# A fused attention and gated MLP on one core: each engine's order worked out in the kernel by a list schedule, with fixed buffers and output stores on the sync engine

## The chip, the cores and the metric

The kernel runs on one core of one Trainium2 chip. Its engines each work through a queue of their own, in order: TensorE (PE) with its weight loads (PEld), VectorE (DVE), ScalarE (ACT), GpSimd (POOL) and SyncE (SP), which only issues transfers here. They wait for each other by semaphores. The metric is the device time of the whole program in microseconds (us), the median of the runs; 770.14 us before the change.

## The reference

```python
xn = layernorm(A_x)                          # 2048 tokens x 1024, bfloat16
qkv = xn @ wqkv                              # 32 heads of 32
# each token sees itself and 7 earlier ones, 2 apart (positions below 0 masked)
s = softmax(q . k_window * 32**-0.5) @ v_window @ wo
g = silu((silu(xn @ w1) * (xn @ w3)) @ w2)   # w1, w3: 1024 x 3584, w2: 3584 x 1024
out = A_x + s * g
```

## The kernel before

The 2048 tokens are four chunks c of 512 (`CH`), in two halves b of two chunks each. One half goes through: projections `qkv(c0)`, the MLP's first layer `mlp_up` in 14 steps fb of 256 hidden columns, with `attention(c0)`, `qkv(c1)` and `attention(c1)` put in among them, then the second layer `mlp_down`, then `wo(c0)`. `wo(c1)` of the first half comes after `qkv(2)` of the second.

- **LayerNorm.** Rows of x are normalised on DVE (`ln_norm`) or on ACT (`ln_norm_act`), transposed by PE (`ln_tp`, banks `tp`) and copied to `xT`.
- **Projection.** `qkv` takes three weight pairs of 2 x 1 MB (`wt`) and makes 8 banks of 8 matmuls from each; ACT evicts them to `qo`, `kT` and `vT`. `kT` and `vT` hold one chunk and 16 older columns, which POOL copies over (the halo) once the attention of the chunk before no longer reads them.
- **MLP.** Both layers use Strassen's scheme in Winograd's form on 2 x 2 blocks: seven products where eight would be needed, with sums of inputs (`xn_sums`, and the down stage's `s1t` to `s4t`), of weights (`w_sums`, `w2_sums`, made on DVE in the first half, stored to `s_dram` and `t_dram` by POOL's queue and loaded again later) and of products. In an up step PE runs groups of four matmuls into banks `ua`, `ue`, `ub`: two of each block product; ACT copies `ua` to a fresh bank (`fork`) and banks to buffers (`snap`); DVE adds, and multiplies gate by value. The last product of each pair, the *tail*, waits in `pend` and is run by `flush()` after the next step's first two products (or directly, at the end of a run of steps). DVE's `h_sb` sum of line 383 has to be through with the bank before the tail adds to it.
- **Attention.** DVE multiplies q by shifted k (`p_t`) and adds over 4 x 2 blocks into `E`; 16 small transfers from POOL's queue regroup `E` into `L` (line 244); DVE and ACT make the softmax (`z`, `zm`, `zs`, `pb`); 16 more transfers bring `pb` back into `E` (line 264); DVE multiplies by shifted v and adds, into `qo`.
- **Down.** `mlp_down` forms seven products per group g of 128 tokens in banks `da`, `db`, `de`: with w2's blocks (`w`) and its stored sums `T1` to `T4`. In the first half, ACT normalises the next half's x (`ln_norm_act`) and PE transposes it between products.
- **Output.** `wo` runs 8 matmuls a group, DVE multiplies by the gate (`o_t`, line 541) and adds x (`x_e`, line 542), and ACT's queue stores the result (line 543).

The buffers are rotating pools: six of 8 KB a partition (`r8`) for all weights and x, three (`att`) for attention, eight of 2 KB (`k2`), and all eight PSUM banks. The framework's scheduler sets the order of each engine's queue from the program order, with `tc.high_priority()` and `tc.issue_after` as hints, at build time. When a buffer comes free decides when a load can be issued: a load on SP waits for the last reader of its buffer, and everything behind it on SP waits too. A step's loads are asked for one step ahead (`up_load(b, fb + 1)`), also by the last step ahead of `qkv(c1)`.

Of the kernel before, what the change touches and what calls it, by code (L numbers as in the profile page):

```python
# [8 lines left out]
FP32 = mybir.dt.float32  # L9
# [4 lines left out]
AX = mybir.AxisListType  # L14
# [3 lines left out]
def kernel(  # L18
# [11 lines left out]

# [24 lines left out]
    NR = 4  # L55
    scale = float(Dh) ** -0.5
# [8 lines left out]

# [4 lines left out]
    psum = ctx.enter_context(tc.tile_pool(name="psum", bufs=8, space=bass.MemoryType.PSUM))  # L70
    small = ctx.enter_context(tc.tile_pool(name="small", bufs=4))
    keep = ctx.enter_context(tc.tile_pool(name="keep", bufs=1))
# [7 lines left out]
    eps_t = const.tile([P, 1], FP32, name="eps_t")  # L80
    nc.vector.memset(eps_t[:], 1e-5)
    scr = const.tile([P, 1], FP32, name="scr")
    nc.scalar.activation(out=scr[:], in_=eps_t[:], func=ACTF.Sqrt)
    ident = const.tile([P, P], BF16, name="ident")
# [5 lines left out]
    maskb = const.tile([P, W, HALO], FP32, name="maskb")  # L90
# [5 lines left out]

    kT = keep.tile([P, NJ, HALO + CH], BF16, name="kT")
    vT = keep.tile([P, NJ, HALO + CH], BF16, name="vT")
    nc.gpsimd.memset(kT[:, :, 0:HALO], 0.0)
    nc.gpsimd.memset(vT[:, :, 0:HALO], 0.0)  # L100
    h_sb = keep.tile([P, FT, BL], BF16, name="h_sb")
    h16 = h_sb[:].bitcast(FP16)
    E = keep.tile([P, W, CH], BF16, name="E")
    qo = keep.tile([P, 2, NJ, CH], BF16, name="qo")
    xT = keep.tile([P, 2, KT, CH], BF16, name="xT")
    xT16 = xT[:].bitcast(FP16)
    xs = keep.tile([P, 4, KH, CH], FP16, name="xs")
    xsb = xs[:].bitcast(BF16)

    warm = k2.tile([P, CH], BF16, tag="k2", name="warm")  # L110
    nc.vector.memset(warm[:], 0.0)
    for i in range(8):
        wps = psum.tile([P, CH], FP32, tag="mm", name=f"warm{i}")
        for _ in range(2 if i < 4 else 1):
            nc.tensor.matmul(wps[:], lhsT=warm[:, 0:P], rhs=warm[:], start=True, stop=True)

    def mm_prod(ps, lhs, rhs, first):
        n = len(lhs)
        for k in range(n):
            nc.tensor.matmul(  # L120
                ps[:], lhsT=lhs[k], rhs=rhs[k], start=(first and k == 0),
                stop=(k == n - 1), skip_group_check=not first,
            )

    def bank(name):
        return psum.tile([P, CH], FP32, tag="mm", name=name)

    def fork(name, src):
        dst = bank(name)
        with tc.high_priority():  # L130
            nc.scalar.copy(out=dst[:], in_=src[:])  # L131
        return dst

    def snap(name, src):
        dst = k2.tile([P, CH], FP32, tag="k2", name=name)
        with tc.high_priority():
            nc.scalar.copy(out=dst[:], in_=src[:])
        return dst

    def ln_norm(c, sts, xt4):  # L140
        n = len(sts)
        mv = small.tile([P, n, nc.vector.BN_AGGR_DIM], FP32, tag="mv")
        rstd = small.tile([P, n], FP32, tag="rstd")
        for i, st in enumerate(sts):
            g = c * NST + st
            nc.sync.dma_start(out=xt4[:, st, :], in_=x_flat[g * P:(g + 1) * P, :])
            stats = small.tile([P, 2, nc.vector.BN_STATS_DIM], FP32, tag="stats")
            for h in range(2):
                nc.vector.bn_stats(out=stats[:, h, :], in_=xt4[:, st, h * 512:(h + 1) * 512])
            nc.vector.bn_aggr(out=mv[:, i, :], in_=stats[:])  # L150
        nc.scalar.activation(out=rstd[:], in_=mv[:, :, 1], func=ACTF.Sqrt, bias=eps_t[:], scale=1.0)
        nc.vector.reciprocal(out=rstd[:], in_=rstd[:])
        for i, st in enumerate(sts):
            nc.vector.tensor_scalar(
                out=xt4[:, st, :], in0=xt4[:, st, :], scalar1=mv[:, i, 0:1], scalar2=rstd[:, i:i + 1],
                op0=ALU.subtract, op1=ALU.mult,
            )

    def ln_norm_act(c, sts, xt4):
        n = len(sts)  # L160
        v = small.tile([P, 4, n], FP32, tag="v")
        for i, st in enumerate(sts):
            g = c * NST + st
            x_t = xt4[:, st, :]
            nc.sync.dma_start(out=x_t, in_=x_flat[g * P:(g + 1) * P, :])
            junk = k2.tile([P, D], BF16, tag="k2", name=f"junk{c}_{st}")
            nc.scalar.activation(out=junk[:], in_=x_t, func=ACTF.Copy, scale=-1.0 / D, accum_out=v[:, 0, i:i + 1])
            nc.scalar.activation(out=junk[:], in_=x_t, func=ACTF.Square, bias=v[:, 0, i:i + 1], accum_out=v[:, 1, i:i + 1])
        nc.scalar.activation(out=v[:, 2], in_=v[:, 1], func=ACTF.Sqrt, bias=eps_t[:], scale=1.0 / D)
        with tc.high_priority():  # L170
            nc.vector.reciprocal(out=v[:, 2], in_=v[:, 2])
            nc.vector.tensor_mul(v[:, 3], v[:, 0], v[:, 2])
        for i, st in enumerate(sts):
            x_t = xt4[:, st, :]
            nc.scalar.activation(out=x_t, in_=x_t, func=ACTF.Identity, bias=v[:, 3, i:i + 1], scale=v[:, 2, i:i + 1])

    def ln_tp(c, st, xt4, copy=nc.scalar.copy):
        for kh in range(2):
            tp = bank(f"tp{c}_{st}_{kh}")
            for k in range(KH):  # L180
                kt = kh * KH + k
                nc.tensor.matmul(  # L182
                    tp[:, k * P:(k + 1) * P], lhsT=xt4[:, st, kt * P:(kt + 1) * P], rhs=ident[:],
                    start=(k == 0), stop=(k == KH - 1), skip_group_check=True,
                )
            copy(
                out=xT[:, c % 2, kh * KH:(kh + 1) * KH, st * P:(st + 1) * P],
                in_=tp[:].rearrange("p (k t) -> p k t", k=KH),
            )

    def ln_transpose(c, group=2, fast=False):
        xt4 = r8.tile([P, NST, D], BF16, tag="r8", name=f"x{c}")
        for st0 in range(0, NST, group):
            (ln_norm_act if fast and st0 == 2 else ln_norm)(c, range(st0, st0 + group), xt4)
        for st in range(NST):
            ln_tp(c, st, xt4, nc.vector.tensor_copy if fast and st == NST - 1 else nc.scalar.copy)

    def qkv(c, mid=None):
        half = c % 2
        if c > 0:  # L200
            nc.gpsimd.tensor_copy(out=kT[:, :, 0:HALO], in_=kT[:, :, CH:CH + HALO])
            nc.gpsimd.tensor_copy(out=vT[:, :, 0:HALO], in_=vT[:, :, CH:CH + HALO])
        for t in range(3):
            wts = []
            for hf in range(2):
                wt = r8.tile([P, 4, D], BF16, tag="r8")
                nc.sync.dma_start(out=wt[:], in_=wqkv_r[:, hf * 4:(hf + 1) * 4, t * D:(t + 1) * D])
                wts.append(wt[:].rearrange("p k (c j) -> p k j c", j=NJ))
            for j in range(NJ):
                ps = bank(f"qkv{c}_{t}_{j}")  # L210
                mm_prod(ps, [wts[kt // 4][:, kt % 4, j, :] for kt in range(KT)],
                        [xT[:, half, kt, :] for kt in range(KT)], True)
                if t == 0:
                    dst = qo[:, half, j, :]
                elif t == 1:
                    dst = kT[:, j, HALO:HALO + CH]
                else:
                    dst = vT[:, j, HALO:HALO + CH]
                with tc.high_priority():
                    nc.scalar.copy(out=dst, in_=ps[:])  # L220
            if t == 0 and mid is not None:
                mid()

    def tree(t, z, op):
        op(t[:], z[:, 0:4, :], z[:, 4:8, :])
        op(t[:, 0:2, :], t[:, 0:2, :], t[:, 2:4, :])
        op(t[:, 0:1, :], t[:, 0:1, :], t[:, 1:2, :])

    def attention(c):
        qT = qo[:, c % 2]  # L230
        for w in range(W):
            o = HALO - DIL * w
            pr = []
            for jh in range(2):
                p_t = att.tile([P, 4, CH], BF16, tag="a4")
                nc.vector.tensor_mul(p_t[:], qT[:, jh * 4:jh * 4 + 4, :], kT[:, jh * 4:jh * 4 + 4, o:o + CH])  # L236
                pr.append(p_t)
# [4 lines left out]
        for r in range(NR):  # L242
            for sq in range(4):
                nc.gpsimd.dma_start(  # L244
                    out=L[r // 2][sq * 32:(sq + 1) * 32, r % 2, :, :], in_=E[r:P:NR, :, sq * P:(sq + 1) * P],
                )
# [348 lines left out]
```

## Time and profile before

| what | us |
|---|---|
| median of 3 runs | 770.14 (769.59 to 772.39) |
| span of the profiled execution | 766.9 |
| PE in work | 749.4 (98%) |
| DVE in work | 602.1 (79%) |
| ACT in work | 321.1 (42%) |
| waits of PE, largest: `qkv` for weights | 4.4, three times |
| `ua` for ACT's copy | 2.9, once |
| mean granted TensorE clock | 0.990 |

The page gives the profiled execution's span, from its first to its last instruction, and no time of its own beside it; it lies 3.2 us under the median of the runs. Busy time of PE counts a matmul from its start to its modelled end, and neighbours overlap by about 0.17 us, so the distance from start to start is what tells its pace. The idle time in brackets at a row of the timeline stands ahead of that row, with what ended it.

### The profile page before, as it was taken

The page shows a single profiled execution, that of the slowest core. Times are in us where ns is not written, and L with a number is a line of the kernel's source. Part 1 is how long each engine was busy: PE and PEld are TensorE (multiplying, and loading weights), DVE is VectorE, ACT ScalarE, POOL GpSimd, SP SyncE. Part 2 cuts the span into 40 slices and gives each one's busy share as a digit, 9 for nine tenths or more (in the row PEclk, how much of TensorE's full clock was granted, in tenths as well). Part 3 has the DMA queues.
Part 4 walks back from the last instruction along what each step waited for, and adds up shares of the span by engine and source line. Part 5 has one row for each costly group of instructions (what it writes and reads, how often), then busy time and mean ns, then how long its engine had stood idle before and what let it go on. Part 6 is the DMA issues. An engine that isn't in the chain of part 4 may idle for free.

```text
span 766.9 us, 9404 instructions
## 1 busy us (share of the span) xinstructions
PE 749.4 (98%) x3516; PEld 375.6 (49%) x3516; DVE 602.1 (79%) x828; ACT 321.1 (42%) x534; POOL 97.2 (13%) x172
## 2 busy tenths in 40 slices
PE   7999999999899999999999899999999999999997
PEld 4664444444565444445566344444466544444443
DVE  6479988887998999150799998565995995924997
ACT  5536444654225489264033044464433444321200
POOL 0000042132000001413000004040000004040000
PEclk8999999999999999999999999999999999999999
DMA  9633799898753668658853836565535257464634
GB/s 331 217 111 108 234 302 272 275 285 297 261 189 83 218 227 268 172 190 262 261 179 103 270 114 169 175 195 165 187 115 201 98 172 207 157 196 147 200 100 140
DMA packets 123117, 150.56 MB, mean 196 GB/s; under 512 B 6080, under 2 KB 97728, under 8 KB 119488
## 3 DMA queue, kind: packets, MB, share of 16 engines
q1 hardware_dynamic: 110336, 115.36, 48.2%
q0 software_dynamic: 8128, 30.42, 11.7%
q10 hardware_dynamic: 4608, 4.20, 1.6%
q8 instruction: 27, 0.44, 0.3%
q14 instruction: 18, 0.15, 0.1%
HBM read 115.34 MB, written 26.21 MB: 185 GB/s over the span
## 4 chain that ended last, share of the span: by engine, by line
PE 86%; DVE 8%; DMA 4%; issue 1%; ACT 1%; SPq 0%; DVEq 0%; ACTq 0%
PE ub L120 18%; PE qkv L120 15%; PE ue L120 12%; PE ua L120 12%; PE db L120 9%; PE de L120 6%; PE da L120 6%; PE s L120 5%; DMA wt<-in_A_wqkv_dram 2%; DVE B L286 1%; DVE B L272 1%; DVE qo L287 1%; DVE p_t L236 1%; PE tp L182 1%; DVE C L272 1%
## 5 line engine op out<-in xcount | busy, mean ns | idle before, releaser
L120 PE MATMUL qkv<-xT,wt 128*128 128x512 bf16 x768 | 169.9, 383 | 4.9 <-DMA wt<-in_A_wqkv_dram 4.4
L120 PEld LDWEIGHTS <-wt 128*128 128x128 bf16 x768 | 110.1, 144 | 63.8 <-DMA wt<-in_A_wqkv_dram 5.8
L120 PEld LDWEIGHTS <-st 128*128 128x128 f16 x896 | 87.7, 98 | 107.4 <-issue 1.7
L120 PE MATMUL ua<-xT,w 128*128 128x512 bf16 x448 | 106.7, 381 | 2.9 <-ACT ub L131 2.9
L120 PEld LDWEIGHTS <-w 128*128 128x128 bf16 x672 | 65.9, 98 | 84.0 <-issue 5.9
L120 PE MATMUL ub<-xs,st 128*128 128x512 f16 x448 | 106.7, 381 | 0.0
L120 PEld LDWEIGHTS <-h_sb 128*128 128x128 bf16 (+1 forms) x672 | 65.5, 98 | 77.5 <-issue 0.5
L236 DVE TENSOR_TENSOR p_t<-qo,kT 128x2048 bf16<-128x2048 bf16 x64 | 77.5, 1215 | 8.5 <-ACT kT L220 8.5
L120 PE MATMUL db<-wt,h_sb 128*128 128x512 f16 x336 | 73.7, 379 | 0.0
L374 DVE TENSOR_TENSOR us<-ue,us 128x512 f32<-128x512 f32 x56 | 37.5, 685 | 38.3 <-PE ue L120 38.3
L120 PE MATMUL s<-wot,qo 128*128 128x512 bf16 x256 | 55.7, 379 | 0.0
L367 ACT ACTIVATE h_sb<-ua 128x512 bf16<-128x512 f32 x56 | 33.3, 598 | 53.3 <-PE ua L120 53.3
L385 ACT ACTIVATE sg<-us 128x512 bf16<-128x512 f32 x56 | 34.8, 630 | 46.7 <-DVE us L374 46.7
L120 PE MATMUL ub<-xs,w 128*128 128x512 f16 x224 | 53.4, 379 | 0.9 <-DVE h_sb L383 0.9
L120 PE MATMUL ue<-xs,st 128*128 128x512 f16 x224 | 52.9, 379 | 0.1
L120 PE MATMUL ue<-xT,st 128*128 128x512 bf16 x224 | 52.9, 379 | 0.0
L131 ACT COPY ub<-ua 128x512 f32<-128x512 f32 x56 | 31.6, 570 | 44.4 <-PE ua L120 25.4
L120 PE MATMUL da<-wt,h_sb 128*128 128x512 bf16 x224 | 49.2, 379 | 0.3 <-DMA wt<-in_B_w_dram 0.3
L264 POOL DMA_DIRECT2D E<-pb x64 | 36.8, 582 | 92.9 <-DVE pb L261 89.1
L397 DVE TENSOR_TENSOR h_sb<-h_sb,ub 128x512 bf16<-128x512 bf16 x56 | 37.0, 679 | 14.4 <-PE ub L120 14.4
L244 POOL DMA_DIRECT2D L<-E x64 | 37.0, 586 | 59.3 <-DVE E L240 55.6
L220 ACT CAST qo<-qkv 128x512 bf16<-128x512 f32 x32 | 18.6, 585 | 61.3 <-PE qkv L120 45.0
(103 smaller groups left out, 841.1 us busy)
## 6 DMA issues: line engine op xcount, KB each, us to landing
wt<-in_A_wqkv_dram SPq DMA_DIRECT2D x24, 1024.0 KB, 7.1
w<-in_B_w_dram SPq DMA_DIRECT2D x42, 512.0 KB, 5.1
s_dram<-st POOLq DMA_DIRECT2D x14, 1024.0 KB, 5.9
wt<-t_dram SPq DMA_DIRECT2D x16, 896.0 KB, 5.4
st<-s_dram SPq DMA_DIRECT2D x14, 1024.0 KB, 5.3
wt<-in_B_w_dram SPq DMA_DIRECT2D x12, 896.0 KB, 6.1
wot<-in_A_wo_dram SPq DMA_DIRECT2D x8, 1024.0 KB, 7.9
w2q<-in_B_w_dram SPq DMA_DIRECT2D x14, 512.0 KB, 3.8
```

The source lines that it names most:

```text
L120: nc.tensor.matmul(ps[:], lhsT=lhs[k], rhs=rhs[k], start=(first and k == 0), stop=(k == n - 1), skip_group_check=not first,)
L131: nc.scalar.copy(out=dst[:], in_=src[:])
L182: nc.tensor.matmul(tp[:, k * P:(k + 1) * P], lhsT=xt4[:, st, kt * P:(kt + 1) * P], rhs=ident[:], start=(k == 0), stop=(k == KH - 1), skip_ ...
L220: nc.scalar.copy(out=dst, in_=ps[:])
L236: nc.vector.tensor_mul(p_t[:], qT[:, jh * 4:jh * 4 + 4, :], kT[:, jh * 4:jh * 4 + 4, o:o + CH])
L244: nc.gpsimd.dma_start(out=L[r // 2][sq * 32:(sq + 1) * 32, r % 2, :, :], in_=E[r:P:NR, :, sq * P:(sq + 1) * P],)
L264: nc.gpsimd.dma_start(out=E[r:P:NR, :, sq * P:(sq + 1) * P], in_=pb[sq * 32:(sq + 1) * 32, :, :],)
L272: nc.vector.tensor_mul(dst, E[:, w, :].unsqueeze(1).to_broadcast([P, 4, CH]), vT[:, js, o:o + CH])
L367: nc.scalar.activation(out=h_sb[:, fl[i], 0:CH], in_=pa[i][:], func=ACTF.Silu)
L374: m = nc.vector.tensor_add(su2[i][:], pe[i][:], su2[i][:])
L385: nc.scalar.activation(out=sg2[i][:], in_=su2[i][:], func=ACTF.Silu)
L397: nc.vector.tensor_mul(h_sb[:, fl[i], 0:CH], h_sb[:, fl[i], 0:CH], pb[i][:])
```

## The change

All operations become records of a `Plan` written in program order: engine, a closure that emits it, the cells it reads and writes, an estimated duration and latency. `place` gives every buffer use a fixed buffer (the one free longest, by program order), `depend` collects what waits for what, `limits` works back from PE's unhindered pace to the latest start of each operation, and `simulate` runs a list schedule: PE in program order, the other four engines each taking, among what is ready by the estimates, the one with the earliest limit. The operations are then emitted in that order, in a mode in which the framework leaves it as it is.

With it come edits by hand. Output stores go from ACT's queue to SP's. The step ahead of `qkv(c1)` no longer loads the step behind it: the second pair of projection weights is asked for ahead of the first product, and the next up step's tiles after the second. Tails are flushed after two groups of the next projection or of the down stage. In `mlp_down` the product with T1 comes ahead of that with T3, and the transposes of one x chunk stand among T3's groups, those of the other in one run ahead of T4. `x_e` is loaded two groups ahead in program order. At the start the third row block of x0 is loaded first, and each row block of x1 gets a square root of its own. Twelve warm-up matmuls remain.

The core of the diff, cut:

```diff
+    def place(self):
+        free = {p: [(-1, i, None) for i in range(len(b))] for p, b in self.pools.items()}
...
+            free[p].sort(key=lambda f: f[:2])
+            _, s.buf, s.prev = free[p].pop(0)
...
+    def limits(self):
+        t = 0.0
+        for o in self.ops:
+            o.limit = None
+            if o.eng == PE:
+                o.limit = t
+                t += o.occ
+        for o in reversed(self.ops):
+            lim = [self.ops[s].limit - self.hop(o, self.ops[s]) for s in o.succ]
+            lim = min(lim) if lim else t
+            d = o.occ + o.lat
+            if o.nbytes:
+                d = o.occ + 2.6 + o.nbytes / 3e5
...
+    def simulate(self):
...
+                i = min((i for i in ready[e] if ops[i].ready <= T), key=lambda i: (ops[i].limit, i))
...
+            if o.nbytes:
+                pipe = max(pipe, T + occ + 0.9) + o.nbytes / 3e5
+                o.done = pipe + 1.3
...
-    r8 = ctx.enter_context(tc.tile_pool(name="r8", bufs=6))
-    att = ctx.enter_context(tc.tile_pool(name="att", bufs=3))
-    k2 = ctx.enter_context(tc.tile_pool(name="k2", bufs=8))
+    plan.pools = {
+        "r8": [const.tile([P, 4 * D], BF16, name=f"r8_{i}") for i in range(6)],
+        "att": [const.tile([P, 4 * CH], BF16, name=f"a4_{i}") for i in range(3)],
+        "k2": [const.tile([P, CH], FP32, name=f"k2_{i}") for i in range(8)],
+        "mm": [psum.tile([P, CH], FP32, name=f"mm{i}") for i in range(8)],
+    }
+    ctx.enter_context(tc.manual_schedule())
...
+    def dma(eng, name, o, a, rd, wr, kb, late=0.0):
+        e = {SP: nc.sync, POOL: nc.gpsimd, ACT: nc.scalar}[eng]
+        occ = {SP: 0.45, POOL: 0.58, ACT: 0.55}[eng]
...
+    def qkv_t(c, t, wts):
+        half = c % 2
+        for j in range(NJ):
+            if j == 2:
+                flush()
...
-            if fb + 1 < FB:
-                up_load(b, fb + 1)
+        if fb + 1 < FB and (b, fb + 1) not in tiles and fb + 1 != cut[b]:
+            up_load(b, fb + 1)
...
+        for g in G:
+            if b + 1 < NB:
+                ln_tp(2 * b + 2, g, xn[0])
+            prod(pb[g], g, 1, 0, rhs, False, FP16)
+            tt("dsa", add, lambda g=g: f32(sp5[g]), pb[g].ap, lambda g=g: f32(sp5[g]), [pb[g], sp5[g]], [sp5[g]], 512, False)
...
-                    nc.scalar.dma_start(out=out_flat[g0:g0 + P, cols], in_=x_e[:, 1])
+            dma(SP, "out", lambda g0=g0, dh=dh: out_flat[g0:g0 + P, dh * CH:(dh + 1) * CH],
+                lambda x=x: b16(x)[:, CH:D], [(x, 1)], [], 128)
...
         attention(c0)
-        flush()
-        qkv(c1)
-        mlp_up(b, range(cut[b], FB))
-        flush()
+        halo(c1)
+        wq = qkv_load(0)
+        wk = qkv_load(1)
+        qkv_t(c1, 0, wq)
+        wv = qkv_load(2)
+        qkv_t(c1, 1, wk)
+        up_load(b, cut[b])
+        if b == 0:
+            w_sums(cut[b])
+        qkv_t(c1, 2, wv)
+        for fb in range(cut[b], FB):
+            up_step(b, fb)
         attention(c1)
         mlp_down(b)
         wo(c0)
     wo(2 * NB - 1)
+    plan.run()
```

In the new code `fork` and the copies are `cp`, DVE's sums `tt` with names: `ua2` (line 374's), `uh` (383's), `um` (397's), `dsa` (505's).

More of the change, by code (lines that the diff above doesn't have):

```diff
@@ L13, with __init__, ap @@
 ALU = mybir.AluOpType
-AX = mybir.AxisListType
+PE, DVE, ACT, POOL, SP = range(5)
+class Slot:
+    def __init__(self, plan, pool, name):
+        self.plan, self.pool, self.name = plan, pool, name
+        self.first = self.last = None
+        self.prev = None
+        self.buf = None
+    def ap(self):
+        return self.plan.pools[self.pool][self.buf][:]
+class Op:
+    __slots__ = ("eng", "emit", "rd", "wr", "occ", "lat", "table", "nbytes", "pred", "succ", "n",
+                 "start", "done", "ready", "limit", "name", "late", "idx")
@@ L17 @@
+LAST = []
 @with_exitstack
@@ L108 @@
[L108 to L117, printed above, removed]
-        n = len(lhs)
[L119 to L140, printed above, removed]
+    warm = plan.pools["k2"][7][:].bitcast(BF16)
@@ new lines, with bank, mm, emit @@
+    nc.vector.memset(warm[:, 0:CH], 0.0)
+    for i in range(12):
+        nc.tensor.matmul(plan.pools["mm"][i % 8][:], lhsT=warm[:, 0:P], rhs=warm[:, 0:CH], start=True, stop=True)
+    MM, TP = 0.2158, 0.0558
+    def bank(name):
+        return plan.slot("mm", name)
+    def mm(ps, lhs, rhs, first, rd, last=True):
+        n = len(lhs)
+        def emit():
+            for k in range(n):
+                nc.tensor.matmul(
+                    ps.ap(), lhsT=lhs[k](), rhs=rhs[k](), start=(first and k == 0),
+                    stop=(last and k == n - 1), skip_group_check=not (first and last),
+                )
+        plan.op(PE, "mm " + ps.name, emit, rd, [ps], n * MM, 0.0)
@@ new lines, in tt, with cp, silu @@
+    def tt(name, fn, o, a, b, rd, wr, n, fast, late=0.0):
+        occ = n / (1920.0 if fast else 960.0) + 0.068
+        plan.op(DVE, name, lambda: fn(out=o(), in0=a(), in1=b()), rd, wr, occ, 0.08, late=late)
+    add, sub, mul, mx = (nc.vector.tensor_add, nc.vector.tensor_sub, nc.vector.tensor_mul, nc.vector.tensor_max)
+    def cp(name, o, a, rd, wr, occ=0.48):
+        plan.op(ACT, name, lambda: nc.scalar.copy(out=o(), in_=a()), rd, wr, occ, 0.11)
+    def silu(name, o, a, rd, wr, occ):
+        plan.op(ACT, name, lambda: nc.scalar.activation(out=o(), in_=a(), func=ACTF.Silu), rd, wr, occ, 0.11,
+                table="silu")
@@ new lines, in ln_act @@
+        plan.op(ACT, f"sq{c}", lambda: nc.scalar.activation(
+            out=v[:, 2, 0:n], in_=v[:, 1, 0:n], func=ACTF.Sqrt, bias=eps_t[:], scale=1.0 / D),
+            [sm + (1, i) for i in range(n)], [sm], 0.2, table="sqrt")
+        plan.op(DVE, f"rc{c}", lambda: nc.vector.reciprocal(out=v[:, 2, 0:n], in_=v[:, 2, 0:n]), [sm], [sm], 0.1)
+        plan.op(DVE, f"nm{c}", lambda: nc.vector.tensor_mul(v[:, 3, 0:n], v[:, 0, 0:n], v[:, 2, 0:n]),
+                [sm] + [sm + (0, i) for i in range(n)], [sm], 0.09)
@@ L178, in ln_tp @@
+        for i, st in enumerate(sts):
+            plan.op(ACT, f"nrm{c}_{st}", lambda i=i, st=st: nc.scalar.activation(
+                out=xrow(xt, st), in_=xrow(xt, st), func=ACTF.Identity, bias=v[:, 3, i:i + 1],
+                scale=v[:, 2, i:i + 1]), [sm], [(xt, st)], 1.15)
+    def ln_tp(c, st, xt, eng=ACT):
+        half = c % 2
         for kh in range(2):
             tp = bank(f"tp{c}_{st}_{kh}")
[L180 to L196, printed above, removed]
@@ L198, in qkv @@
-    def qkv(c, mid=None):
-        half = c % 2
[L200 to L204, printed above, removed]
-            for hf in range(2):
[L206 to L227, printed above, removed]
+            def emit(kh=kh, tp=tp):
+                for k in range(KH):
+                    kt = kh * KH + k
+                    nc.tensor.matmul(
+                        tp.ap()[:, k * P:(k + 1) * P], lhsT=xrow(xt, st)[:, kt * P:(kt + 1) * P], rhs=ident[:],
+                        start=(k == 0), stop=(k == KH - 1), skip_group_check=True,
+                    )
@@ new lines, in ln_tp, with qkv_load @@
+            plan.op(PE, f"tp{c}_{st}", emit, [(xt, st)], [tp], KH * TP, 0.0)
+            fn = nc.scalar.copy if eng == ACT else nc.vector.tensor_copy
+            plan.op(eng, f"xT{c}_{st}", lambda kh=kh, tp=tp: fn(
+                out=xT[:, half, kh * KH:(kh + 1) * KH, st * P:(st + 1) * P],
+                in_=tp.ap().rearrange("p (k t) -> p k t", k=KH)),
+                [tp], xt_cells(half, kh, st), 0.48 if eng == ACT else 0.6, 0.11)
+    def qkv_load(t):
+        wts = []
+        for hf in range(2):
+            wt = plan.slot("r8", f"wqkv{t}_{hf}")
+            dma(SP, f"wqkv{t}_{hf}", lambda wt=wt: wt.ap().rearrange("p (k d) -> p k d", k=4),
+                lambda hf=hf: wqkv_r[:, hf * 4:(hf + 1) * 4, t * D:(t + 1) * D], [], [wt], 1024)
+            wts.append(wt)
+        return wts
@@ new lines, in qkv_w, with halo @@
+    def qkv_w(wt, k, j):
+        return lambda: wt.ap().rearrange("p (k c j) -> p k j c", k=4, j=NJ)[:, k, j, :]
+    def halo(c):
+        for nm, b in (("k", kT), ("v", vT)):
+            plan.op(POOL, f"halo{nm}", lambda b=b: nc.gpsimd.tensor_copy(
+                out=b[:, :, 0:HALO], in_=b[:, :, CH:CH + HALO]),
+                [(nm, j) for j in range(NJ)], [(nm, j, "halo") for j in range(NJ)], 0.95)
+    def qkv_t(c, t, wts):
+        half = c % 2
+        for j in range(NJ):
+            if j == 2:
+                flush()
+            ps = bank(f"qkv{c}_{t}_{j}")
+            for hf in range(2):
+                mm(ps, [qkv_w(wts[hf], k, j) for k in range(4)],
+                   [lambda k=k, hf=hf: xT[:, half, hf * 4 + k, :] for k in range(4)], hf == 0,
+                   [wts[hf]] + xt_cells(half, hf), last=hf == 1)
+            if t == 0:
+                dst, wr = (lambda j=j: qo[:, half, j, :]), qo_cells(half, [j])
+            elif t == 1:
+                dst, wr = (lambda j=j: kT[:, j, HALO:HALO + CH]), [("k", j)]
+            else:
+                dst, wr = (lambda j=j: vT[:, j, HALO:HALO + CH]), [("v", j)]
+            cp(f"ev{c}_{t}_{j}", dst, ps.ap, [ps], wr)
@@ L302 @@
+    bx = {(r, kh): [lambda k=k, r=r, kh=kh: xT[:, r, kh * KH + k, :] for k in range(KH)] for r in range(2) for kh in range(2)}
+    tx = [[lambda k=k, i=i: xs[:, i, k, :] for k in range(KH)] for i in range(4)]
+    tiles = {}
     pend = []
@@ new lines, in rhs_load, with prod @@
+                res.append((wt, [lambda k=k, v=v: v()[:, k, :] for k in range(NQ)]))
+            return res
+        def prod(ps, g, row, fh, rhs, first, dt):
+            src = h_sb if dt == BF16 else h16
+            for q, (wt, ops) in enumerate(rhs):
+                fs = range(fh * FH + q * NQ, fh * FH + (q + 1) * NQ)
+                mm(ps, [lambda f=f: src[:, f, gs[row][g]] for f in fs], ops, first and q == 0,
+                   [wt] + h_cells(fs, row, [g]), last=q == 1)
+        s1v = lambda g: xT16[:, g // 2].rearrange("p k n -> p (k n)")[:, 0:FH * 256].rearrange(
+            "p (f n) -> p f n", f=FH)[:, :, (g % 2) * P:(g % 2 + 1) * P]
@@ L547 @@
+    cut = (11, 10)
+    x0 = plan.slot("r8", "x0")
+    for st in range(NST):
+        x_load(0, st, x0)
+    ln_dve(0, 0, x0)
+    ln_dve(0, 1, x0)
+    ln_act(0, [2], x0)
+    ln_dve(0, 3, x0)
+    for st in range(NST):
+        ln_tp(0, st, x0, DVE if st == NST - 1 else ACT)
     for b in range(NB):
         c0, c1 = 2 * b, 2 * b + 1
-        qkv(c0, partial(ln_transpose, 1) if b == 0 else None)
+        if b:
+            halo(c0)
+        qkv_t(c0, 0, qkv_load(0))
+        if b == 0:
+            x1 = plan.slot("r8", "x1")
+            for st in range(NST):
+                x_load(1, st, x1)
+            for st in range(NST):
+                ln_dve(1, st, x1)
+        wk = qkv_load(1)
+        if b == 0:
+            for st in range(NST):
+                ln_tp(1, st, x1)
+        qkv_t(c0, 1, wk)
+        qkv_t(c0, 2, qkv_load(2))
```

712 lines of the change are left out of this document (436 added, 276 removed).

## The prediction, made before the changed kernel was run

> **What bounds the kernel now.** I read four views. The page first:
>
> ```profile
> span 766.9 us, 9404 instructions
> ...
> PE 749.4 (98%) x3516; PEld 375.6 (49%) x3516; DVE 602.1 (79%) x828; ACT 321.1 (42%) x534; POOL 97.2 (13%) x172
> ```
>
> PE is in work almost all the time, so the first question is what its work costs unhindered. The chain of what ended last has "29.77 27.64 PE qkv L120 x128": 0.2159 us a matmul of 512 columns. The 32 transposes of x1 fill 27.82 to 29.61, 0.056 us each. After the first projection starts (13.08) there are 3376 matmuls and 96 transposes: 728.9 + 5.4 = 734.3 us, which would end at 747.4. The last matmul ends at 762.8 (27.79 us from 734.98), so 15.4 us are lost, and 4.1 us of epilogue and last store follow.
>
> Where the 15.4 us lie is read from PE's timeline, stage start against stage start at that pace:
>
> ```profile
> 186.85 1.89 PE L120 MATMUL ub<-xs,st 128*128 128x512 f16 x8
> 189.07 1.89 PE L120 MATMUL ub<-xs,w 128*128 128x512 f16 x8 [0.33 <-DVE h_sb L383]
> 194.50 19.82 PE L120 MATMUL qkv<-xT,wt 128*128 128x512 bf16 x83 [3.55 <-DMA wt<-in_A_wqkv_dram]
> 214.70 14.03 PE L120 MATMUL qkv<-xT,wt 128*128 128x512 bf16 x64 [0.37 <-DMA wt<-in_A_wqkv_dram]
> 229.21 9.93 PE L120 MATMUL qkv<-xT,wt 128*128 128x512 bf16 x45 [0.47 <-DMA wt<-in_A_wqkv_dram]
> ```
>
> This is qkv(1), after the 11th up step. The tail is 0.56 late (with a small slip before it), then PE waits from 190.80 (189.07 + 8 x 0.2159) to 194.50, 3.70, for weights. From 194.50 to the next stage at 238.98 are 44.48 us where 192 matmuls need 41.45: 3.03 more. The first 83 matmuls alone take 19.82 less one overlapping end of 0.17, 1.7 over their 17.9. In all 7.3 us.
>
> The other place is the start of the second half (PE, then ACT):
>
> ```profile
> 435.98 1.89 PE L120 MATMUL ue<-xs,st 128*128 128x512 f16 x8
> 440.79 2.76 PE L120 MATMUL ua<-xT,w 128*128 128x512 bf16 x8 [2.92 <-ACT ub L131]
> 443.34 2.75 PE L120 MATMUL ub<-xs,st 128*128 128x512 f16 x8
> 445.93 1.89 PE L120 MATMUL ue<-xT,st 128*128 128x512 bf16 x8
> ```
> ```profile
> 430.14 9.93 ACTq L543 DMA_DIRECT2D out_dram<-x_e  x7
> 440.17 1.06 ACT L131 COPY ub<-ua 128x512 f32<-128x512 f32 x2 [18.95 <-DVE o_t L541]
> ```
>
> PE lacks the bank copy `fork` for 3.09 us, because ACT stands at output stores that wait for DVE; then 16 matmuls take 5.14 (440.79 to 445.93) instead of 3.45, 1.69 more. A tail at 559.81 is 0.5 late: 5.28 in all. The rest: 0.92 in the first projection (14.74 for 64, need 13.82), 0.64 at steps 11 to 13, 0.42 in `da`, 0.68 where transposes of x2 and x3 lie among `de` and `db`, 0.12 elsewhere.
>
> **The change, part by part.** It removes no matmul: 3516 before and after, and DVE's 784 tensor operations stay. So the sum is one of waits.
>
> Loads regrouped. Up step 10 no longer loads step 11's tiles, and all six `wqkv` loads are asked for as buffers come free. In the new SP order the first goes out when tail 8 ends, the second when step 9's sums are used: at PE's pace 19.0 and 13.0 us ahead of their matmuls; the other four are 15.5 to 24 us ahead. One lands in 7.1 us in the DMA rows. So 3.70 goes, and 3.03 with it (0.84 of named waits, 1.7 of slow matmuls, the rest small waits after them). Step 11's weights follow 27.6 us ahead. What is late next there is DVE: 19.97 and 19.86 of 20 us busy in the windows at 200 and 220. But DVE has only to free vT, whose last reader ended at 228.3 and is followed by POOL's halo copy of 1.12. If the third projection starts 7 us earlier, at 222, its evictions wait until 229.5 and PE fills free banks of 1.73 us each meanwhile; with eight of them no wait. I take -6.73; if that cover is gone, up to 7 comes back (rival B).
>
> Tails (`flush`) now come after two groups of the next projection, or two of `da`, 16 or 28 matmuls, where the old one followed directly. Their `uh` sum is 0.68 of DVE: -0.56 at 189, -0.5 at 559.
>
> Stores on SP. 32 issues (about 0.45 each, as SP's other small ones) leave ACT, where seven held 9.93 us. The wait on DVE goes with them: behind a store on SP stand `x_e` loads and the second half's up weights. In the new order those are asked for at least 20.7 us ahead at PE's pace, land in 5.3, and a store waits for one group (1.73) and two DVE sums (1.37). So the fork comes when its matmuls end, -4.78. The small rows of `x_e` (3.0 us to land) are asked for four to five groups ahead, 7 us or more.
>
> [...]
>
> `da`: its second half loads 7.6 us ahead against a landing of 6.1: -0.3. Steps 11 to 13: DVE order changes, -0.4 of 0.64 (0 to -0.64). Transposes: x3's eight groups now stand in one run, 0.22 us each on PE but an ACT copy of about 0.5 each, with four banks free; four copies too late for PE, so 1.0 instead of 0.68: +0.3 (-0.5 to +1.5).
>
> Start: x0's third row is loaded first, for ACT. But DVE now does six statistics (0.64) before any normalisation; the last row arrives at 6.46 as before, so the first transposes come at about 9.05 instead of 8.49. They run without the gaps of 0.29, and only four ACT copies (0.5) instead of five precede the first projection: it starts at 13.1 to 13.6, +0.2 (-0.5 to +1.0).
>
> PE's slow matmuls after a long wait need a word. After 3.55 and 2.92 us of idling, 1.7 us more were spent each time (16 matmuls at 0.32 after the second), and the granted clock is 0.91 in the windows 180 to 200 and 440 to 460, against 1.00 in those around; after 0.47 nothing is seen. So I count 1.7 with each wait near 3 us that goes or comes. [...]
>
> Sum: -6.73 - 0.56 - 4.78 - 0.5 - 0.3 - 0.4 + 0.3 + 0.2 = -12.8 us. New small waits: 0 to 3, I take 0.3, since every PE consumer keeps two groups of distance: **-12.5**. The page gives the span alone, 766.9; it becomes 754.4. The median of the runs (770.14, from 769.59 to 772.39) has 3.2 more outside the span, which no part of this touches: **757.6 us**.
>
> **Rivals.** A, slower: a gather holds the engines in order. Attention sends 16 small DMAs each way, through eight semaphores in turn, so the ninth waits for the first:
>
> ```profile
> L<-E POOLq DMA_DIRECT2D x64, 64.0 KB, 4.5
> E<-pb POOLq DMA_DIRECT2D x64, 64.0 KB, 4.6
> ```
>
> At 0.58 an issue, eight take 4.64, so 4.6 just fits. The new order puts the PV products on DVE about where the last of them should land, with `dsa` and ACT's silus behind. In the first down stage the way from the last score is 13.9 (16 x 0.58 + 4.6), 10 of softmax on DVE and ACT, 13.2 for the way back, and 6 for four products, an add and the first `dsa`: 43 us. PE comes to T4 after 50 (224 matmuls and 32 transposes), and wants ACT's transposed copies some 4 earlier: 3 us of slack. With a landing of l, four rounds of eight are each l - 4.6 late, so PE waits from l = 5.4 on. At 7.5 it waits 11.6 - 3 and 1.7 for the clock, 10.3; in the other three chunks the two gathers are 5.8 late each, against 3.3 by which `uh` is covered, 5 a chunk: 25 us in all, 783. It turns slower than before from about l = 6.8. Against it: the old trace's second z sum, which needs twelve gathers, began 11.6 after the first was issued, in a busy stretch; 4.6 fits that. A mild form, l = 6, costs 4.3: 762.
>
> B, DVE takes the place of the weights in qkv(1): it has 164 of 180 us busy from 60 to 240, and 16.2 us of idling behind gathers in the whole run. If it stands there again, the evictions of vT are that late and 7 comes back: 764.6. For it, the two windows; against it, 13.8 us of banks.
>
> C, the stores hold SP at the second half's start, by DVE's backlog, and the up weights come late: 4.8 back, 762.4. Against it, the 20.7 us.
>
> D, the new order isn't one in effect: queues meet the same events as before and the waits stay: 770. Against it, the loads are really in another order.
>
> **Numbers.** My case 0.70 (755 to 761), mild A or B or C 0.14 (762 to 766), the same 0.07 (D, or A at its turn), slower A 0.09. So the likeliest is 757.6. The low end takes every lost term but the cold one and a start 0.5 better: 770.1 - 14.4 - 0.5 = 755.2, and 0.7 for the scatter of the runs: 754.5. The high end takes in the mild cases and the edge of D: 768. About 0.5%, 3.85 us, is what runs that differ by up to 2.8 can tell from none. Faster 0.82, within 0.10, slower 0.08 (a part of A ends at the edge).
>
> **What would show it.** Right: PE waits for `wqkv` and for ACT's fork gone from its list; no matmul group after 14 us at 0.32; stage distances of 12.1 us for an up step throughout; the last matmul at about 750. ACT's queue without `out_dram`. Wrong: waits of PE behind DVE's `uh`, `um` or `dsa` with a releaser that is a gather (A), behind ACT's vT (B), or behind `w`, `st` (C). A start after 14 would spoil that term alone.

## The result, and the profile after

The changed kernel took 759.9 us (median of 4 runs, 759.13 to 761.14) where the kernel before took 769.87 beside it: a ratio of 0.987, 95% interval 0.9845 to 0.9895. The forecast was 757.6. The span of the profiled execution fell from 766.9 to 757.6, 9.3 where the sum had 12.5. The page:

```profile
span 757.6 us, 9366 instructions
...
PE 742.4 (98%) x3457; PEld 375.8 (50%) x3516; DVE 599.4 (79%) x830; ACT 320.1 (42%) x535; POOL 106.8 (14%) x172
```

All buffers are named by pool now (`r`, `a`, `k`, `mm`), and a line is a helper's. The two places of the old loss, in PE's timeline (start, duration, operation, in brackets the idle time ahead):

```profile
190.88 1.89 PE L299 MATMUL mm<-xs,r 128*128 128x512 f16 x8
192.61 39.88 PE L299 MATMUL mm<-xT,r 128*128 128x512 bf16 x180
...
437.18 1.89 PE L299 MATMUL mm<-xT,r 128*128 128x512 bf16 x7
438.91 1.89 PE L299 MATMUL mm<-xs,r 128*128 128x512 f16 x8
```

The tail stands among the first groups of qkv(1), which runs on without a wait; the second half's first step has no gap. From 28.57 to 327.29 PE does 1384 matmuls in 298.72 us, at 0.2159 each 298.80: nothing is lost. From 361.21 to the end of the last matmul at 753.33 (725.54 + 27.79), less the 0.17 by which a last end stands out, it is the same: 391.95 for 1816 (392.07). All but 0.1 of what PE still loses after its start lies between:

```profile
341.16 1.46 PE L421 MATMUL mm<-ident,r 128*128 128x128 bf16 x16
345.75 1.84 PE L421 MATMUL mm<-ident,r 128*128 128x128 bf16 x16 [3.13 <-ACT xT L428]
347.44 13.94 PE L299 MATMUL mm<-r,h_sb 128*128 128x512 f16 x56
361.21 13.98 PE L299 MATMUL mm<-r,qo 128*128 128x512 bf16 x62
```

The 56 matmuls and 64 transposes from 327.29 to 347.44 take 20.15 us instead of 15.67, and the 56 of T4 after the wait 13.77 instead of 12.09: 6.16 in all, where the forecast had 1.0. DVE's timeline tells why:

```profile
327.49 0.69 DVE L308 TENSOR_TENSOR k<-mm,k 128x512 f32<-128x512 f32 x1 [2.33 <-PE mm L299]
335.87 1.23 DVE L308 TENSOR_TENSOR qo<-E,vT 128x2048 bf16<-128x2048 bf16 x1 [7.69 <-DMA E<-a]
337.01 0.68 DVE L308 TENSOR_TENSOR k<-mm,k 128x512 f32<-128x512 f32 x1
```

DVE stands 7.69 us at the first PV product until the second gathers have landed. The row at 337.01 is the first `dsa`, whose matmuls ended at 330.8. ACT's silu and its copies of the transposes follow `dsa` in order, and PE lacks banks. This is rival A's chain.

### The profile page after: what moved, and what is told of

Its sections match the earlier page's. It is cut to its first block, busy times and chain, and to the rows that moved or that the text cites. A ratio compares the mean times of both kernels' runs of the same rounds, so it can differ in the third digit from the quotient of the medians.

```text
span 757.6 us, 9366 instructions
## 1 busy us (share of the span) xinstructions
PE 742.4 (98%) x3457; PEld 375.8 (50%) x3516; DVE 599.4 (79%) x830; ACT 320.1 (42%) x535; POOL 106.8 (14%) x172
## 4 chain that ended last, share of the span: by engine, by line
PE 84%; DVE 5%; ACT 4%; DMA 3%; issue 2%; POOL 2%; SPq 0%; DVEq 0%; ACTq 0%
PE mm L299 83%; DVE a L308 3%; DMA a<-E 2%; POOL E L322 1%; ACT k L396 1%; ACT k L399 1%; DMA E<-a 1%; DVE k L308 1%; DVE r L308 1%; DVE h_sb L308 1%; PE mm L421 1%; POOL a L322 1%; DVE small L379 0%; ACT xT L428 0%; DMA r<-in_A_x_dram 0%
## 5 line engine op out<-in xcount | busy, mean ns | idle before, releaser
L299 PEld LDWEIGHTS <-r 128*128 128x128 bf16 (+1 forms) x2336 | 263.4, 113 | 241.1 <-issue 0.7
L299 PE MATMUL mm<-xT,r 128*128 128x512 bf16 x1395 | 322.9, 379 | 2.8 <-ACT xT L428 0.5
L299 PE MATMUL mm<-xs,r 128*128 128x512 f16 x896 | 207.7, 379 | 0.0
L299 PE MATMUL mm<-r,h_sb 128*128 128x512 f16 (+1 forms) x664 | 147.8, 382 | 0.4
L308 DVE TENSOR_TENSOR a<-qo,kT 128x2048 bf16<-128x2048 bf16 x64 | 76.6, 1217 | 39.7 <-ACT kT L313 39.6
L308 DVE TENSOR_TENSOR a<-a,a 128x2048 bf16<-128x2048 bf16 (+1 forms) x72 | 87.6, 1217 | 19.4 <-DMA a<-E 19.0
L313 ACT COPY k<-mm 128x512 f32<-128x512 f32 x128 | 74.4, 586 | 55.8 <-PE mm L299 55.3
L308 DVE TENSOR_TENSOR a<-E,vT 128x2048 bf16<-128x2048 bf16 x56 | 66.0, 1215 | 0.0
L308 DVE TENSOR_TENSOR k<-mm,k 128x512 f32<-128x512 f32 x72 | 48.0, 683 | 20.0 <-PE mm L299 18.0
L299 PE MATMUL mm<-r,qo 128*128 128x512 bf16 x250 | 55.4, 379 | 0.3
```

The lines of the kernel that those rows point to most:

```text
L299: nc.tensor.matmul(ps.ap(), lhsT=lhs[k](), rhs=rhs[k](), start=(first and k == 0), stop=(last and k == n - 1), skip_group_check=not (first ...
L308: plan.op(DVE, name, lambda: fn(out=o(), in0=a(), in1=b()), rd, wr, occ, 0.08, late=late)
L313: plan.op(ACT, name, lambda: nc.scalar.copy(out=o(), in_=a()), rd, wr, occ, 0.11)
```

## The experiments

Each of the twelve has its own time, with the kernel before timed beside it.

| run | what | us | ratio to before, 95% |
|---|---|---|---|
| | the changed kernel | 759.9 | 0.987 (0.9845 to 0.9895) |
| e1 | `dsa` ahead of the products | 754.55 | 0.9796 (0.9773 to 0.9818) |
| e2 | short T4 loads | 755.48 | 0.9807 (0.9784 to 0.983) |
| e3 | stores back on ACT | 760.8 | 0.9875 (0.9851 to 0.9898) |
| e4 | preload restored | 776.34 | 1.0083 (1.0059 to 1.0107) |
| e8 | tails at once | 763.47 | 0.9906 (0.9872 to 0.994) |
| | **from the kernel before** | | |
| e5 | stores on SP | 769.71 | 0.9997 (0.9967 to 1.0028) |
| e6 | loads regrouped | 779.51 | 1.0119 (1.0076 to 1.0162) |
| e7 | both | 776.44 | 1.0082 (1.0055 to 1.0109) |
| e10 | gathers in one run | 774.39 | 1.0074 (1.005 to 1.0099) |
| e9 | e7 and e10 | 766.13 | 0.9958 (0.9938 to 0.9978) |
| e12 | e9, stores on ACT | 769.18 | 0.9998 (0.998 to 1.0015) |
| e11 | e9, vT's halo copy on ACT | 764.06 | 0.9939 (0.9917 to 0.996) |

The rows come from several sittings, between which the kernel before's own median went from 769.1 to 770.4. A difference of two rows is good to about 1 us.

**e1, what the wait is.** In `Plan.run`, ahead of `simulate`:

```diff
+        first = [o for o in self.ops if o.name == "dsa"][:2]
+        for pv in [o for o in self.ops if o.name == "pv1"]:
+            for o in first:
+                pv.pred.add(o.idx)
+                o.succ.append(pv.idx)
```

> The changed kernel, with the first PV products of the second attention put behind the first two dsa sums in DVE's order (20 rows of DVE's order and 4 of SP's move, nothing else). Theory A: PE's 3.13 us wait at the x3 transposes, and the 1.68 us that the next 56 matmuls take over their pace, come from DVE, which stands at its first product until the gathers have landed (7.69 us, until 335.87) with dsa behind it, and from ACT's silu and copies behind dsa. Then the wait falls under 1 us, the slow matmuls go, and the time falls by 4 to 4.8: 755.1 to 755.9. Theory B: the wait is the copies' own rate, eight groups in one run at about 0.5 us a copy against 0.22 us a group on PE, as the forecast had it; then at least 2.5 us of it stay and the time is 759 to 760.

It took 754.55. DVE does the two sums as their matmuls end, and PE has no wait there:

```profile
331.20 0.69 DVE L313 TENSOR_TENSOR k<-mm,k 128x512 f32<-128x512 f32 x1 [2.78 <-PE mm L304]
334.67 0.69 DVE L313 TENSOR_TENSOR k<-mm,k 128x512 f32<-128x512 f32 x1 [2.77 <-PE mm L304]
337.16 1.23 DVE L313 TENSOR_TENSOR qo<-E,vT 128x2048 bf16<-128x2048 bf16 x1 [1.80 <-DMA E<-a]
```
```profile
341.40 2.91 PE L426 MATMUL mm<-ident,r 128*128 128x128 bf16 x32
344.15 12.25 PE L304 MATMUL mm<-r,h_sb 128*128 128x512 f16 x56
```

T4 is back at pace, 12.09 us, and the stretch from the first transpose at 327.53 to 344.15 is 0.95 over its pace. So theory A holds, and theory B's copies cost what the forecast gave them, 1.0. This is the fastest version, 15.7 us (2.0%) below the kernel before.

**e2, why the gathers were late.** The T4 loads of the first half are cut to one slice of seven:

```diff
-                    dma(SP, "t2", v, lambda q=q: t_dram[:, q * NQ:(q + 1) * NQ, t, :],
+                    m = 1 if short else NQ
+                    dma(SP, "t2", lambda v=v, m=m: v()[:, 0:m], lambda q=q, m=m: t_dram[:, q * NQ:q * NQ + m, t, :],
```

> The changed kernel in its order, but the loads of T4's weights in the first half fetch one of seven slices each (128 instead of 896 KB, twice); T4 of that half then multiplies leftovers. Theory A1: the second gathers land late (5.9 us from the last issue to the first product) because these loads share the DMA engines with them (share 1.01 to 1.06 from 329 to 335). Then the first product comes at 332.5 to 333.5, DVE's dsa and ACT follow, PE's wait falls from 3.13 under 1 us and the time to 755 to 756.5. Theory A2: the landing is the gathers' own, sixteen through eight semaphores; then the first product stays at 335 to 336 and the time at 759 to 760.

The first product came at 333.46, the wait went, and the time was 755.48. A1 holds: these loads shared the DMA engines with the gathers. In the changed kernel, where the DMA share is 1.03 from 329 to 335, the first T4 load is issued at 326.27; the nine gathers issued ahead of it landed in 2.2 to 3.0 us, the seven behind it in 5.6 to 6.2. In e2 DVE stood 4.00 us at the first product instead of 7.69.

The kernel before has the same spread: in this chunk the medians of its two batches are 2.3 and 2.2 us, with the DMA share at 0.44 and 0.47 in their first 6 us, but the slowest of each batch, beside weight loads, took 7.3. PE had no wait from them there.

**e3 and e4, the two hand-made parts undone in the list's order.**

```diff
-            dma(SP, "out", lambda g0=g0, dh=dh: ...
+            dma(ACT, "out", lambda g0=g0, dh=dh: ...
```

> The changed kernel with its 32 output stores on ACT's queue again, placed there by the same list schedule. Theory Q, the queue's: any store on ACT holds the bank copies behind it, so PE's wait of about 3 us at the second half's first ub product returns with 1.7 of slow matmuls: 764 to 765. Theory O, the order's: the list puts six of the eight stores of wo(1) ahead of the first fork, and the sixth row is ready 0.7 us after the fork's matmuls ended, where PE comes to the copied bank 4.1 us after them. Then no wait, 759.5 to 761.

Theory O: 760.8, within the scatter of 759.9. The first fork came 2.94 us after the step's first matmul (431.24 to 434.18) instead of 1.06, and still in time. In the list's order the queue of the stores hardly matters.

```diff
-        if fb + 1 < FB and (b, fb + 1) not in tiles and fb + 1 != cut[b]:
+        if fb + 1 < FB and (b, fb + 1) not in tiles:
```

with `w_sums` likewise, and each third of `wqkv` loaded ahead of its use.

> The changed kernel with the old rule of the loads: up steps 10 (first half) and 9 (second half) load the next step's tiles again, and each third of wqkv is asked for just ahead of its use. If the forecast's terms hold, PE waits about 3.7 us for wqkv at the start of qkv(1) and loses some 3 us within it: +6 to +7.5, 766 to 767.5. The rival is that the list's order alone would have kept the weights in time, with DVE's sums for step 11 moved later: then under 1.5 us, 759.5 to 761.5.

It cost 16.4 net, more than twice the forecast's term, in PE's list of waits:

```profile
PE mm L299 <- DMA r<-in_A_wqkv_dram: 14.8, 3, 5.3
```

Each third of qkv(1) waits 4.5 to 5.3, with slow matmuls after it, where the kernel before had 3.55 and twice under 0.5. The slow matmuls come to 6.8 us more; the net cost is less than the sum because the wait at the transposes, with its slow matmuls, is gone from this run. I read the three waits so: two of the six `r` buffers hold step 11's tiles, and the fixed places leave each next pair none in time; that was not tried.

**e5 to e7, the same two parts alone in the old order.** Line 543 on `nc.sync` (e5); `and fb + 1 != cut[b]` in `mlp_up`, `wqkv` asked for two thirds at a time and step 11's tiles with the last third (e6); both (e7).

> The kernel before, with its 32 output stores on SP instead of ACT and nothing else edited (some sums of the output rows change places on DVE). If the store term of the forecast holds, PE's 2.92 us wait for the fork and the slow matmuls after it go: -4.8, a ratio of 0.994 and about 765. Rival C: the stores wait on SP with the second half's loads behind them, and the wait comes back as one for w or st: within 1 us of before.

> The kernel before, with the loads alone regrouped: the steps 10 (first half) and 9 (second) no longer load the next step's tiles, those follow with the last third of qkv, and wqkv is asked for two thirds at a time. If the load term holds, PE's wait of 3.55 us for wqkv goes, with most of the 3.03 us lost after it: -5.5 to -7, a ratio of 0.991 to 0.993. After the restored preload cost the changed kernel 16 us, the rival is that the regrouping only works with fixed buffers: then less than 2 us.

> The kernel before with both edits, the stores on SP and the loads regrouped, and its old order otherwise. If the two terms add, -10.3 to -11.8: 758 to 760, the changed kernel's time without any list schedule. Rival: the list schedule brought part of the gain, and this stays at 762 or above.

No gain, 9 us slower, 6 us slower: e5 has its rival's number, and its mechanism only in small part; e6 and e7 missed both. In e5 the fork's wait is gone, and one of the same size stands at the next tail, since DVE's old order has scores and output sums ahead of `uh`:

```profile
451.01 2.42 PE L120 MATMUL ub<-xs,w 128*128 128x512 f16 x8 [3.02 <-DVE h_sb L383]
```

The small part of rival C: on SP the loads of `x_e` now stand behind stores. DVE waits 1.18 us for one at 438.92, and at the end of the program, where the two alternate on SP, the span runs 5.4 us past the last matmul instead of 4.1.

In e6 qkv(1) runs without a wait, and then rival B comes, at up step 11 (PE, POOL, ACT, DVE):

```profile
245.04 3.57 PE L120 MATMUL ua<-xT,w 128*128 128x512 bf16 x8 [11.88 <-ACT vT L232]
```
```profile
194.67 0.59 POOL L276 DMA_DIRECT2D E<-pb  x1
236.36 8.01 POOL L202 COPY vT<-vT 128x128 bf16<-128x128 bf16 x1 [41.10 <-DVE C L284]
```
```profile
244.40 4.01 ACT L232 CAST vT<-qkv 128x512 bf16<-128x512 f32 x8 [24.43 <-POOL vT L202]
```
```profile
202.98 1.23 DVE L284 TENSOR_TENSOR qo<-E,vT 128x2048 bf16<-128x2048 bf16 x1 [9.18 <-DMA E<-pb]
```

The last of sixteen gathers is issued at 194.67, as POOL has each batch behind a step's weight stores, which wait for DVE. The products start at 202.98 and release vT at 236.36; POOL's copy takes 8.01, and eight full banks wait for ACT. The rest of e6's loss is mostly the fork's wait at the second half's start, 6.3 us where the kernel before had 2.92, with the stores on ACT as there.

**e9 and e10, the gathers in one run.** The gathers of lines 244 and 264 are put under `tc.high_priority()`, on top of e7 (e9) and alone (e10).

> The kernel before with the stores on SP and the loads regrouped (the last experiment but one, 776.4) and one edit more: the 32 gathers of a chunk's attention get the high priority that the sums for PE have, so POOL issues each sixteen in one run instead of four to six per up step behind the weights' stores. Theory G: the 11.6 us that PE waited at up step 11 come from POOL's order, since the last back gather was issued at 192.53 behind a store that waited for DVE, the products began at 200.36 after 8.68 of idling on DVE and ended at 233.7, POOL's vT copy (8.0) and ACT's eight evictions came after them, and PE had no bank. Then the products begin by 180, the wait goes with its slow matmuls, and the time is 761 to 764. Theory V: DVE is full there anyway (164 of 180 us), the products end as late: 774 to 777.

> The kernel before with that priority of the gathers alone. Its two large waits are for wqkv (3.55) and for the fork behind the stores (2.92), which earlier gathers don't touch: 769 to 771, no difference. The rival is that DVE's backlog stood behind these waits too: then 762 to 766.

e9 is 10.3 below e7 (9.5 by the ratios): theory G in the main. It missed its 761 to 764, since 3.24 of the wait were left. Alone the gathers cost 4.6, which neither theory had: PE's waits for `wqkv` grew from 4.4 to 8.5. I read it as DVE's earlier products delaying step 11's sums (their store was issued at 196.33 after 14.63 of waiting) and so a buffer; that was not tried.

**e11 and e12, the rest of that wait, and the store term by itself.** In e11 `nc.gpsimd.tensor_copy` of vT's halo becomes `nc.scalar.copy`; e12 is e9 without e5's edit.

> The last version of the old order (stores on SP, loads regrouped, gathers in one run: 766.1), with the copy of vT's sixteen columns moved from POOL to ACT; the order on PE, DVE and SP stays as it is. Theory P: what is left of PE's wait at step 11 (3.24 us, and 1.3 of slow matmuls) is the copy itself, 8.61 us on POOL from 226.65 while DVE ran without a pause, where the same copy took 1.12 in the kernel before. On ACT it takes under 1 us, the evictions begin 7 us earlier, and the time falls to 761 to 762.5. Theory D: the evictions wait for DVE's last product anyway: 765.5 to 767.

> The same version with its stores back on ACT (loads regrouped, gathers in one run, vT's copy on POOL), so that the store term stands alone in an order where the sums of the second half's first steps come in time (1.1 and 0.7 us late). If the store term holds there, the fork's wait of about 3 us returns with 1.7 of slow matmuls, less the 1.8 named: +2.5 to +3.5, 768.5 to 769.5. Against it: moving the stores gained nothing alone, since DVE's sums took the place; then 765.5 to 767.

On ACT the copy takes 0.30, and the wait is gone:

```profile
226.54 0.30 ACT L202 COPY vT<-vT 128x128 bf16<-128x128 bf16 x1 [7.02 <-DVE C L284]
```

The gain is 2.1 by the medians, not 3.6 to 5, and the intervals of e9 and e11 overlap: 0.98 and 1.06 of new waits for DVE's sums came at 245. Theory P for the wait, with part of the time given back. e12 is 3.1 above e9, the size expected: eight stores stand on ACT ahead of the fork. The parts are not the expected ones. The fork's wait is 4.55 us instead of about 3; the wait of 3.24 at step 11, the same in both, is followed by 1.1 more of slow matmuls; and about 1.6 comes back at the end, where e9 has 5.7 us after the last matmul and e12 4.1.

```profile
427.98 12.48 ACTq L557 DMA_DIRECT2D out_dram<-x_e  x8
```
```profile
441.18 3.08 PE L120 MATMUL ua<-xT,w 128*128 128x512 bf16 x8 [4.55 <-ACT ub L131]
```

**e8, the tails.** Both `flush()` calls go ahead of their loops.

> The changed kernel with the tails flushed at once, ahead of the next projection and of da, where it has two groups first. If the forecast's tail terms hold, the tails at 188 and at 552 come 0.5 us late each: about +1, 760.4 to 761.4. The rival is that DVE's list order now has the sums in time: no difference.

It is 3.6 above the changed kernel (2.8 by the ratios). PE has four waits for `uh`, 1.5 in all, longest 0.7; 0.67 of the rest is a later start (the second transposes at 27.45 against 26.78), which an edit at 186 cannot cause, and about 1 stays open. The tail term holds: 0.17 and 0.71 at the two tails that it names, 0.9 for its 1.06, and 0.6 more at the two ahead of `da`.

## Why the prediction was right, and where it was not

**The number** is right to 2.3 us, partly by luck. One term of the sum is far off, and smaller errors the other way took back more than half of it: PE loses 6.17 after its start, forecast 2.7. Too low was the stretch of the transposes, 6.16 for 1.0 (+5.2). Too high were the start (12.86 for 13.28, -0.4), the first projection's cold clock (0.10 for 0.92, -0.8; from 12 to 15 us 0.82 was granted, in the kernel before 0.50), and small waits that did not come (-0.9). With 0.17 more after the last matmul that makes the span's +3.2, to rounding. Outside the span the median adds 2.3 for 3.2. That 3.2 was no constant: each run's own record has its time 2.0 to 2.2 us above its span before the change and 1.7 to 1.8 after, so about 1.1 of it was the profiled execution lying below the median.

**The step that failed** is rival A's slack, "3 us", with l = 4.6. The chain to the first product was costed at 37.1 (13.9 + 10 + 13.2) and took 42.9, from the last score sum's end at 292.94 to 335.87. The first gathers took 19.3 to the last z sum instead of 13.9, the softmax about 9 instead of 10, the second gathers 14.5 instead of 13.2. The median 4.6 mixed quiet and busy stretches, while the chain hangs on the last gather of a batch. The old trace showed that: its second z sum, read as fitting 4.6, needs twelve gathers, and the other four of that batch took 6.2 to 7.3. Now loads for T1, for w2's next block and for T4 fall on the two batches; the first one's median was 5.7, and the first product came 5.9 after the last issue of the second.

A's mild form was priced at 4.3 for l = 6; 3.13 of wait and 1.68 of slow matmuls are 4.8. So the wait and its price were right and its chance too small. The rounds of eight were only half right: POOL waited for landings within the first batch (1.96 us ahead of the ninth gather) but issued all sixteen of the second in one run of 9.15. e1 shows that the transposes themselves were sized right (0.95).

**Loads regrouped, -6.73:** it came in full, and e4 shows that the changed kernel needs the regrouping. But the reason why nothing takes its place, banks worth 13.8 us, was not the one that carries. In the old order the next thing late, DVE and POOL at vT, costs 11.9 (e6). The list issues the second gathers from 138.73 to 148.5 and copies vT's halo from 202.57 to 208.86, where the kernel before had them spread over 161.9 to 186.0 and the copy at 227.32. At PE's pace the third projection begins at about 216.8, so vT is free 8 us ahead of it, and B has nothing to wait for. (The 16.2 us of idling that rival B counts behind gathers are one wait for a second batch; the old trace has 10.6 more behind a first one.) In the old order the early gathers alone give back 10.3 (e9, on top of e7).

**Stores on SP, -4.78:** the wait and the slow matmuls went, but they went by the order. Alone it is 0 (e5); with the list it is not needed (e3); it is worth 3.1 net where the old order has all stores ahead of the fork (e12). The waiting stores did hold their queue: SP stood 4.41 us at three of them from 432.12. The up loads behind them went at 437.38, and PE's list of waits names no load, so C did not come.

**Tails, -1.06:** confirmed by e8. **`da` and steps 11 to 13:** no loss is left, so all of 0.42 and 0.64 went instead of 0.3 and 0.4. **Cold first projection:** it is scatter, not the change: its row shows 13.97 us in e10 and e12, which have the old start, 14.65 and 14.71 in e9 and e11, 14.90 before.

**The clock, 1.7 per wait:** it held here: 2.92 (before), 3.02 (e5) and 3.13 us cost 1.69, 1.69 and 1.68. The granted clock was 0.72 from 440 to 446 in the kernel before and 0.50 from 348 to 351 in the changed one. But 1.7 is no fixed price: a wait of 3.24 us cost 1.7 in e9 and 2.8 in e12, and the last section has one that cost nothing.

## What to carry to other kernels

When a wait is removed from an engine that is 98% busy, the gain is what is left after the next late thing; that can be read ahead only by following each in-order queue to its own last release, POOL's gathers and copies included. Parts of such a change need not add: alone they gave 0, +9 and +5 us, together -4, and with every queue reordered -10. A list schedule is only as good as its durations: one estimate for a transfer that landed here in 2.2 to 3.0 us ahead of weight loads and in up to 7.3 beside them put two sums behind a wait of 7.7, and moving them ahead was worth 5 us. For a chain that needs every transfer of a batch, read the slowest and not the median.

## What was not expected of the hardware

POOL's copy of 128 x 128 elements took from 0.29 to 8.61 us. Four long ones (8.61 in e9, 8.01 in e6, 6.94 in e1, 6.29 in the changed kernel) each ended 0.15 us after the end of the first DVE operation whose successor had not begun by then. Two shorter ones of the changed kernel (1.74 and 2.94) ended 0.23 after DVE began one that reads PSUM (`k<-mm,k`), at 451.91 and 547.61. e9's long one, POOL and then the DVE rows at its end:

```profile
226.65 8.61 POOL L202 COPY vT<-vT 128x128 bf16<-128x128 bf16 x1 [21.64 <-DVE C L284]
```
```profile
233.89 1.22 DVE L250 TENSOR_TENSOR p_t<-p_t 128x2048 bf16<-128x2048 bf16 x1
235.14 0.69 DVE L251 TENSOR_TENSOR p_t<-p_t 128x1024 bf16<-128x1024 bf16 x1
```

235.14 is the first start after an end (235.11); all rows from 226.41 on overlap, and the copy ends at 235.26. On ACT it took 0.30 at the same place (e11). So each of the four long copies lasted to the first gap in a chain of overlapping DVE operations. Not every copy does: in the kernel before (POOL, then DVE) it ended where two overlap:

```profile
227.32 1.12 POOL L202 COPY vT<-vT 128x128 bf16<-128x128 bf16 x1 [31.48 <-DVE C L272]
```
```profile
227.08 1.22 DVE L236 TENSOR_TENSOR p_t<-qo,kT 128x2048 bf16<-128x2048 bf16 x1
228.21 1.31 DVE L286 TENSOR_TENSOR B<-B,C 128x2048 bf16<-128x2048 bf16 x1
```

It ended at 228.44, about 0.15 after the end of the first of these, and the second took 1.31 us instead of 1.22. What decides between the two cases is open.

How long a wait must be to bring slow matmuls is not settled by these runs. The waits of 2.92, 3.02 and 3.13 us were followed by 1.7 us of slow matmuls, while 2.84 (e10, at 448.08) and 2.55 (e7, at 457.87) were not. But a shorter one was, in e10 again, 13 matmuls after a wait of 5.28:

```profile
204.90 30.76 PE L120 MATMUL qkv<-xT,wt 128*128 128x512 bf16 x134 [2.78 <-DMA wt<-in_A_wqkv_dram]
```

At their pace the 134 would take 29.10, 1.7 less. So the length of the wait alone does not decide. The mean granted clock of the kernel before, one program, lies between 0.986 and 0.996 beside e5 alone. This suggests that a wait near 3 us is followed by the slow clock at one time and not at another; no two traces here show that of the same wait.
